# Attention with a threshold and a feed-forward block on one core: the plan's order after 47 drawn shifts of its ranks

## The chip, the core and the metric

The kernel runs on one NeuronCore of a Trainium2 chip. The metric is the time of one launch in microseconds (us) of device time. The engines are TensorE (PE in the profile; its weight loads are PEld), VectorE (DVE), ScalarE (ACT), GpSimd (POOL) and SyncE (SP, which here only issues DMAs). Each runs its own row of instructions in the order in which the program was written for it, and semaphores make one engine wait for another.

## The reference

Eight batches of eight heads, 576 positions, head width 64. An attention keeps only those scores that lie within `tau` of their row's maximum; its output, 4608 tokens of width 512, goes through two matrix products of inner width 2048 with `s * relu(h)^2 + b` between them. The inputs q, k, v and w_in are drawn eight times larger than the setup shows.

```python
scores = scale * np.matmul(q, k.transpose(0, 1, 3, 2))
thresh = np.max(scores, axis=-1, keepdims=True) - tau
scores = np.where(scores >= thresh, scores, -1000000000.0)
scores = scores - np.max(scores, axis=-1, keepdims=True)
attn = np.exp(scores)
attn = attn / (np.sum(attn, axis=-1, keepdims=True) + 1e-09)
attn_out = np.matmul(attn, v)
...
h = x @ w_in
r = np.maximum(h, 0.0)
g = s * (r * r) + b
out = g @ w_out
```

## The kernel before

**Attention, by visits and tiles.** A visit is a pair of heads with 256 query rows (half of a batch; in the second half 64 rows more, the tail). There are 64 visits. A visit has four tiles of 128 query rows of one head, with a tail five; tiles are numbered from 0 through the whole run, so tiles 0 to 3 are visit 0, and 16 to 20 visit 4. A tile goes through these steps:

- TensorE makes the scores of the two heads of a tile pair (L368; later visits use split numbers, L379 and L390). They go to one of three PSUM tiles, s0, s1 and o, in turn.
- DVE scales them in place and takes the row's extreme (L411), ACT takes the exponential into a buffer em0, em1, tr0 or tr1 (L422), DVE cuts by the threshold and sums (L425) and takes the reciprocal (L428), POOL multiplies by it (L429).
- In the first eight visits TensorE transposes the result (L439 into the score's own PSUM tile, and four times L441 into the tiles h or pv), and ACT copies it to er (L448, L450). Later DVE transposes (L462, L464), and DMAs carry the blocks to er.
- When all tiles of a visit are in er, TensorE multiplies by the values (L492, into pv), and ACT copies the result into the token block x (L502).

**Feed-forward, by blocks and steps.** Four visits fill a block of 256 tokens (18 blocks, two of them made of the tails). ACT and DVE split it into a high and a low part (L599, L601). Step f of 16 makes one slice of the inner width: twelve products (L615, into h), ReLU and square on ACT (L622, L623), a split into high and low part (ACT L625 and POOL L626, gl), and two times three products with w_out (L632, into o).

**Weights.** Each of the 16 slices of weights is loaded once by DMA as 64-bit words and turned into two 32-bit parts during the first 155 us: ACT L560, DVE L563 and L565, ACT L569, POOL L571, each once for w_in and once for w_out, and a sum on DVE (L574). So the first block's step f can't start before slice f is there.

**The order.** Nothing here is scheduled on the chip. Every operation is handed to a `Plan` (L32) with its engine, a cost, and the keys that it reads and writes. `ordered` (L121) is a list scheduler: it runs a model of the engines and takes on each the ready operation of lowest rank. `run` (L61) tries 18 settings, in eight rounds each; a round schedules forward, then backward from the end, and the backward starts are the next ranks. `worth` plays each forward order with random delays, and the order of the lowest mean wins. The operations are then written in that order, all engines in one list, and from this list the framework derives the semaphore waits. It does so by whole tiles: an operation that touches s0 waits for the last one before it in the list that touched s0, even where the plan's keys keep the two apart (the transposition L439 writes columns of s0 that the scaling L411 does not read).

Of the kernel before, what the change touches and what calls it, by code (L numbers as in the profile page):

```python
# [26 lines left out]
FIRST_WEIGHTS = 4  # L27
SECOND = 3.5
PAIR = 1170


class Plan:  # L32
# [28 lines left out]
    def run(self):  # L61
        ops = self.ops
        after = [[] for _ in ops]
        for n, o in enumerate(ops):
            for d in o[4]:
                after[d].append(n)
        before = [o[4] for o in ops]
        best = None
        for share, later, stretch in [(a, b, c) for a in self.SHARES for b in self.LATER for c in self.STRETCH]:
            rank, early = [o[5] for o in ops], set()  # L70
            for _ in range(ROUNDS):
                more = [(share if n in early else later) * self.SPARE.get(o[0], 0) +
                        (stretch - 1) * o[1] * (o[0] == "PE" and n in early) for n, o in enumerate(ops)]
                busy = [o[1] + s for o, s in zip(ops, more)]
                done = [o[2] + s for o, s in zip(ops, more)]
                order = self.ordered(before, after, rank, busy, done, False)
                worth = self.worth(order)
                if best is None or worth < best[0]:
                    best = worth, order
                early = {n for t, n in order if t < self.EARLY}  # L80
                end = {n: t + done[n] for t, n in order}
                last = max(end.values())
                order = self.ordered(after, before, [last - end[n] for n in range(len(ops))], busy, done, True)
                start = {n: -t - done[n] for t, n in order}
                rank = [start[n] for n in range(len(ops))]
        self.order = best[1]
        return [ops[n][3] for _, n in self.order]

    def worth(self, order):
        return sum(self.played(order, *slow) for slow in self.SLOW) / len(self.SLOW)  # L90
# [100 lines left out]
def tile_attention_ffn(ctx: ExitStack, tc: tile.TileContext, qT, kT, v, tau, w_in, w_out, s, b, out):  # L191
# [56 lines left out]
    def pe(cost, fn, r, w, at, tiled=False):  # L248
        plan.add("PE", (cost, cost + 170), fn, r, w, at, tiled=tiled)
# [101 lines left out]
    def scores(vs, i, t):  # L351
# [11 lines left out]
        def pairs():  # L363
            for hf in range(2):
                cs = slice(hf * HS, (hf + 1) * HS)
                for j in range(2):
                    r = slice(j * D, (j + 1) * D)
                    nc.tensor.matmul(flat[ks[j]][:, S0 + hf * HS:S0 + (hf + 1) * HS], qr[r, n, t * P:(t + 1) * P], kr[r, n, cs],  # L368
                                     start=True, stop=True)
        pe(PAIR, pairs, vs.kq + ["guard"] + (["h0"] if not i else []), ks, i - SCORES_AHEAD, True)  # L370

# [472 lines left out]
```

## Time and profile before

| | us |
|---|---|
| median of 3 runs | 1227.43 |
| lowest and highest | 1227.29, 1227.7 |
| the profiled execution | 1229.16 |
| its span, first to last instruction | 1227.2 |

| engine | busy us | share of the span |
|---|---|---|
| PE | 1198.6 | 98% |
| PEld | 987.3 | 80% |
| DVE | 798.6 | 65% |
| ACT | 765.1 | 62% |
| POOL | 718.3 | 59% |

The profiled execution took 1.96 us more than its span; that lies before the first and behind the last instruction. Share of busy time is over the whole span. A stretch of the run can be limited by another engine than the one that is busiest over the whole. A wait stands in brackets behind an instruction: how long its engine was idle just before it, and what released it.

### The profile page before, as it was taken

The numbers are of one execution on the slowest core, as the hardware profiler recorded it, in microseconds if no ns is written. First come the engines' busy times: TensorE is split into PE (matmuls) and PEld (weight loads), VectorE is DVE, ScalarE is ACT, GpSimd is POOL, SyncE is SP. The second block draws the span as 40 slices with busy tenths as digits, with TensorE's granted clock in tenths as the row PEclk, the third lists the DMA queues.
The fourth block names the chain that finished last, engine by engine and source line by source line (L and its number), as shares of the span: only waits on it lengthen the run. The fifth ranks groups of instructions, "written<-read, shape, count | busy, mean of one in ns | idle before, by whom it ended". The sixth has DMA issues, their size and how long they took to land.

```text
span 1227.2 us, 24552 instructions
## 1 busy us (share of the span) xinstructions
PE 1198.6 (98%) x7926; PEld 987.3 (80%) x7926; DVE 798.6 (65%) x2158; ACT 765.1 (62%) x1890; POOL 718.3 (59%) x822
## 2 busy tenths in 40 slices
PE   7779999999999999999999999999999999999998
PEld 5457777887887888888888888888888888878987
DVE  6897876767777766657676757666666576663021
ACT  5777755666666666656666666666656665654443
POOL 3777745767765775656665665667656676652200
PEclk7899999999999999999999999999999999999999
DMA  7851165777777776676576766566866666752000
GB/s 248 270 194 45 39 152 137 164 185 170 185 169 172 172 171 163 164 166 163 131 178 155 169 155 155 132 156 154 185 146 163 159 156 149 174 134 64 9 18 18
DMA packets 259536, 180.67 MB, mean 147 GB/s; under 512 B 83537, under 2 KB 238161, under 8 KB 259409
## 3 DMA queue, kind: packets, MB, share of 16 engines
q1 hardware_dynamic: 259120, 178.98, 60.1%
q8 instruction: 63, 1.03, 0.4%
q14 instruction: 65, 0.52, 0.1%
q10 hardware_dynamic: 288, 0.13, 0.0%
HBM read 87.03 MB, written 9.44 MB: 79 GB/s over the span
## 4 chain that ended last, share of the span: by engine, by line
PE 93%; DMA 2%; DVE 2%; ACT 1%; issue 1%; POOL 1%; SPq 0%; ACTq 0%; DVEq 0%; POOLq 0%
PE h L615 34%; PE o L632 32%; PE pv L492 13%; PE s L379 9%; PE s L368 2%; PE s L390 1%; PE pv L441 1%; DVE s L411 1%; DMA tau_t<-in_tau_dram 1%; DMA vb<-in_v_dram 1%; DMA qr<-in_q_dram 0%; DMA w<-in_moe_w_out_dram 0%; PE s L357 0%; PE s L439 0%; ACT em L422 0%
## 5 line engine op out<-in xcount | busy, mean ns | idle before, releaser
L615 PE MATMUL h<-xh,w 128*128 128x256 f32 x2304 | 467.1, 284 | 2.5 <-ACT g L622 2.5
L615 PEld LDWEIGHTS h<-xh,w 128*128 128x128 f32 x2304 | 377.5, 190 | 29.4 <-issue 11.2
L632 PE MATMUL o<-w,gh 128*128 128x512 f32 x1152 | 365.5, 399 | 0.6 <-DVE em L652 0.6
L411 DVE TENSOR_SCALAR_CACHE_REDUCE s<-s,nsc 128x576 f32<-128x576 f32 x283 | 230.7, 821 | 161.4 <-PE s L379 123.7
L429 POOL TENSOR_SCALAR em<-em,st,zero 128x576 f32<-128x576 f32 x270 | 229.5, 851 | 178.2 <-DVE st L428 123.2
L615 PE MATMUL h<-xl,w 128*128 128x256 f32 x1152 | 325.2, 282 | 0.6 <-DVE xl L601 0.6
L626 POOL TENSOR_TENSOR gl<-g,gh 128x256 fp32r<-128x256 f32 x272 | 204.0, 751 | 185.5 <-ACT gh L625 164.0
L425 DVE SCALAR_TENSOR_TENSOR em<-s,st,em 128x577 f32<-128x577 f32 x268 | 216.9, 810 | 77.1 <-ACT st L420 48.9
L422 ACT ACTIVATE em<-s,st 128x576 f32<-128x576 f32 x268 | 197.6, 738 | 70.5 <-DVE s L411 44.0
L632 PEld LDWEIGHTS o<-w,gh 128*128 128x128 f32 x1152 | 196.6, 189 | 37.3 <-issue 11.9
L632 PE MATMUL o<-w,gl 128*128 128x512 f32 x576 | 224.7, 390 | 0.6 <-POOL gl L626 0.6
L615 PEld LDWEIGHTS h<-xl,w 128*128 128x128 f32 x1152 | 219.0, 190 | 6.4 <-DVE xl L601 0.8
L622 ACT ACTIVATE g<-h 128x256 f32<-128x256 f32 x288 | 110.2, 383 | 172.4 <-PE h L615 151.5
L462 DVE STREAM_TRANSPOSE tr<-em 128x512 f32<-128x512 f32 x252 | 178.0, 706 | 53.5 <-POOL em L429 42.1
L492 PE MATMUL pv<-er,vb 128*64 128x256 f32 (+1 forms) x1280 | 174.2, 418 | 3.4 <-ACT er L450 3.4
L344 POOL TENSOR_TENSOR k<-kr,k 64x576 fp32r<-64x576 f32 x104 | 148.5, 1429 | 45.6 <-ACT k L343 31.5
L492 PEld LDWEIGHTS pv<-er,vb 128*64 128x64 f32 x1280 | 86.9, 139 | 74.0 <-issue 14.8
L625 ACT CAST gh<-g 128x256 fp32r<-128x256 f32 x288 | 116.3, 404 | 43.3 <-PE o L632 40.2
L379 PE MATMUL s<-k 128*128 128x288 f32 x832 | 142.8, 296 | 0.2
L379 PEld LDWEIGHTS s<-k 128*128 128x128 f32 x832 | 126.9, 188 | 15.2 <-issue 2.1
L632 PEld LDWEIGHTS o<-w,gl 128*128 128x128 f32 x576 | 108.2, 188 | 25.8 <-POOL gl L626 1.3
L623 ACT ACTIVATE g<-g 128x256 f32<-128x256 f32 x288 | 120.0, 417 | 4.3
(104 smaller groups left out, 945.5 us busy)
## 6 DMA issues: line engine op xcount, KB each, us to landing
er<-tr SPq DMA_DIRECT2D x448, 160.0 KB, 3.4
kr<-in_k_dram SPq DMA_DIRECT2D x116, 288.0 KB, 4.2
vb<-in_v_dram SPq DMA_DIRECT2D x128, 128.0 KB, 3.0
qr<-in_q_dram SPq DMA_DIRECT2D x56, 160.0 KB, 4.4
er<-tr SPq DMA_DIRECT2D x112, 80.0 KB, 2.3
w<-in_moe_w_in_dram SPq DMA_DIRECT2D x16, 512.0 KB, 6.0
w<-in_moe_w_out_dram SPq DMA_DIRECT2D x16, 512.0 KB, 6.1
out_dram<-oo SPq DMA_DIRECT2D x30, 256.0 KB, 2.6
```

Of the source, the lines that this page charges most:

```text
L344: pool((1500, 1500), lambda: nc.gpsimd.tensor_tensor(out=z()[D:P], in0=kr[D:P, j], in1=z()[D:P].bitcast(F32), op=ALU.subtract), rk + [("z" ...
L379: nc.tensor.matmul(flat[sk][:, S0 + hf * HS:S0 + (hf + 1) * HS], lazy["q"][:, x, j, qc], lazy["k"][:, j, cs], start=(x == 0), stop=(x == 1))
L411: dve((740, 875), lambda: nc.vector.tensor_scalar(out=ps[:, S0:S0 + S], in0=ps[:, S0:S0 + S], scalar1=nsc, scalar2=None, op0=ALU.mult, op1 ...
L422: act((632, 740), lambda: nc.scalar.activation(out=ev, in_=ps[:, S0:S0 + S], func=AF.Exp, bias=st8[:, 0:1], scale=-1.0), [sk, (ks_, 0)], [ ...
L425: dve((742, 830), lambda: nc.vector.scalar_tensor_tensor(out=eb, in0=ps[:, S0:S0 + S + 1], scalar=st8[:, 1:2], in1=eb, op0=ALU.is_le, op1= ...
L429: pool((795, 825), lambda: nc.gpsimd.tensor_scalar(out=ev, in0=ev, scalar1=st8[:, 4:5], scalar2=zero, op0=ALU.mult, op1=ALU.add), [em_k, ( ...
L462: nc.vector.transpose(out=to[:, :, 0:NQ].rearrange("p m c q -> p m (c q)"), in_=ev[:, 0:M].rearrange("p (m r) -> p m r", m=4))
L492: nc.tensor.matmul(ps[j * D:(j + 1) * D, 0:32 * nb], vb[r, n, j, c], er[r, n, j, 0:nb, 32 * c:32 * c + 32], start=(c == 0), stop=(c == 4))
L615: nc.tensor.matmul(ps, w[:, c, :], x[:, c, :], start=(c == 0 and i == 0), stop=(c == NC - 1 and i == 2))
L623: act((322, 417), lambda: nc.scalar.activation(out=g, in_=g, func=AF.Square), [f"g{k}"], [f"g{k}"], at)
L626: do((712, 740), lambda: eng.tensor_tensor(out=lo, in0=g, in1=hi.bitcast(F32), op=ALU.subtract), [f"g{k}", f"gh{n}"], [f"gl{n}"], at)
L632: nc.tensor.matmul(bank["o"][:, t, :], a[:, ts_], w, start=(f == 0 and i == 0), stop=(f == NF - 1 and i == 2))
```

## The change

The order that won is taken up once more with the ranks that made it. For each of 47 numbers, `shifted` seeds a random generator, draws a width and a start of a stretch of the model's time, some kinds of operations (a kind is an engine, a cost and a place in the code), and a shift; the ranks of the operations of those kinds in that stretch are shifted by it, all alike or each by its own draw. `ordered` makes a new order, and the next number shifts that one. The last order is used without a comparison. Costs, keys, tiles and the operations themselves are the same. A line of the kernel before stands 21 lines further on behind the new function (L411 is L432, L571 is L592).

```diff
+SHIFTS = (0, 20, 48, 103, 150, 205, 238, 276, 352, 398, 411, 419, 421, 471, 481, 540, 551, 662, 694, 892, 1084, 1250,
...
-                    best = worth, order
+                    best = worth, order, rank, busy, done
...
-        self.order = best[1]
+        worth, order, rank, busy, done = best
+        for n in SHIFTS:
+            rank = self.shifted(n, order, rank)
+            order = self.ordered(before, after, rank, busy, done, False)
+        self.order = order
         return [ops[n][3] for _, n in self.order]
+
+    def shifted(self, n, order, rank):
+        draw, end = random.Random(n), order[-1][0]
+        kind = [(o[0], o[1], o[3].__code__.co_firstlineno) for o in self.ops]
+        kinds = sorted(set(kind))
+        width = draw.choice((2e3, 5e3, 15e3, 50e3, 200e3))
+        first = draw.uniform(0, 150e3) if draw.random() < 0.4 else draw.uniform(0, end)
+        some = set(draw.sample(kinds, draw.choice((1, 1, 1, 2, 4)))) if draw.random() < 0.75 else set(kinds)
+        shift, alike = draw.gauss(0, 1) * draw.choice((500, 2000, 6000)), draw.random() < 0.6
+        new = list(rank)
+        for t, m in order:
+            if first <= t < first + width and kind[m] in some:
+                new[m] += shift if alike else draw.gauss(0, 1) * shift
+        return new
```

Each engine still runs the same instructions: 7071 matrix products on PE, of which 1701 stand at another place of its row than before; the first 58 and the last 541 places are unchanged. On DVE 686 of 1584 places differ, on POOL 236 of 827. Three places follow.

DVE in the second visit (tiles 6 to 9 pass through; L563 and L565 convert weights), before:

```order
L425 SCALAR_TENSOR_TENSOR tr0_79,st0_71<-s0_98,st0_71,tr0_79 128x577
L425 SCALAR_TENSOR_TENSOR tr1_80,st1_72<-s1_99,st1_72,tr1_80 128x577
L563 TENSOR_SCALAR xl_172<-xl_172 128x512
L565 SCALAR_TENSOR_TENSOR k_87<-w2_153,k_87 128x512
L565 SCALAR_TENSOR_TENSOR xl_172<-w1_138,xl_172 128x512
L563 TENSOR_SCALAR k_87<-k_87 128x512 x2
L565 SCALAR_TENSOR_TENSOR k_87<-w2_153,k_87 128x512
L411 TENSOR_SCALAR o_100,st2_73<-o_100,nsc_68 128x576
L411 TENSOR_SCALAR s0_98,st3_74<-s0_98,nsc_68 128x576
L416 TENSOR_SCALAR st2_73<-st2_73,tau8_67 128x1
L428 RECIPROCAL st0_71<-st0_71 128x1
L428 RECIPROCAL st1_72<-st1_72 128x1
```

and now:

```order
L446 SCALAR_TENSOR_TENSOR tr0_79,st0_71<-s0_98,st0_71,tr0_79 128x577
L586 SCALAR_TENSOR_TENSOR xl_172<-w1_138,xl_172 128x512
L446 SCALAR_TENSOR_TENSOR tr1_80,st1_72<-s1_99,st1_72,tr1_80 128x577
L449 RECIPROCAL st0_71<-st0_71 128x1
L449 RECIPROCAL st1_72<-st1_72 128x1
L584 TENSOR_SCALAR k_87<-k_87 128x512
L432 TENSOR_SCALAR o_100,st2_73<-o_100,nsc_68 128x576
L586 SCALAR_TENSOR_TENSOR xl_172<-w1_138,xl_172 128x512
L437 TENSOR_SCALAR st2_73<-st2_73,tau8_67 128x1
L432 TENSOR_SCALAR s0_98,st3_74<-s0_98,nsc_68 128x576
```

The block of six conversions that stood between the second visit's cuts and the next scalings is spread out, and the reciprocals of tiles 6 and 7 follow their cuts at once.

PE at the same place (the scores of tiles 8 and 9, the values of visit 0, the transpositions of tiles 5, em1, and 6, tr0), before:

```order
L439 MATMUL s1_99<-k_87,em0_77 64x128
L441 MATMUL h_102<-k_87,em0_77 128x128 x4
L492 MATMUL pv_101<-er_84,vb_83 64x256 x10
L368 MATMUL o_100<-kr_81,qr_82 128x288
L368 MATMUL s0_98<-kr_81,qr_82 128x288
L368 MATMUL o_100<-kr_81,qr_82 128x288
L368 MATMUL s0_98<-kr_81,qr_82 128x288
L439 MATMUL o_100<-k_87,em1_78 64x128
L441 MATMUL pv_101<-k_87,em1_78 128x128 x4
L439 MATMUL s0_98<-k_87,tr0_79 64x128
L441 MATMUL h_102<-k_87,tr0_79 128x128 x4
```

and now:

```order
L460 MATMUL s1_99<-k_87,em0_77 64x128
L462 MATMUL h_102<-k_87,em0_77 128x128 x4
L389 MATMUL o_100<-kr_81,qr_82 128x288
L389 MATMUL s0_98<-kr_81,qr_82 128x288
L389 MATMUL o_100<-kr_81,qr_82 128x288
L389 MATMUL s0_98<-kr_81,qr_82 128x288
L513 MATMUL pv_101<-er_84,vb_83 64x256 x10
L460 MATMUL s0_98<-k_87,tr0_79 64x128
L462 MATMUL h_102<-k_87,tr0_79 128x128 x4
L460 MATMUL o_100<-k_87,em1_78 64x128
L462 MATMUL pv_101<-k_87,em1_78 128x128 x4
```

The scores stand ahead of the values now, and tile 6 is transposed ahead of tile 5.

POOL at the first steps of the first feed-forward block (tiles 18, tr0, 19, tr1, and 20, em0; gl0 and gl1 of steps 0 and 1), before:

```order
L571 TENSOR_TENSOR w7_657<-k_87,w7_657 128x512 x2
L429 TENSOR_SCALAR tr1_80<-tr1_80,st1_72,zero_69 128x576
L429 TENSOR_SCALAR em0_77<-em0_77,st2_73,zero_69 128x576
L626 TENSOR_TENSOR gl0_95<-g0_90,gh0_92 128x256
L626 TENSOR_TENSOR gl1_96<-g1_91,gh1_93 128x256
L571 TENSOR_TENSOR w8_736<-k_87,w8_736 128x512 x2
```

and now:

```order
L592 TENSOR_TENSOR w7_649<-k_87,w7_649 128x512
L647 TENSOR_TENSOR gl0_95<-g0_90,gh0_92 128x256
L647 TENSOR_TENSOR gl1_96<-g1_91,gh1_93 128x256
L450 TENSOR_SCALAR tr1_80<-tr1_80,st1_72,zero_69 128x576
L450 TENSOR_SCALAR em0_77<-em0_77,st2_73,zero_69 128x576
L647 TENSOR_TENSOR gl2_97<-g0_90,gh2_94 128x256
```

The low parts of the first two steps stand ahead of the multiplications of tiles 19 and 20.

## Rows read from the trace of the kernel before

**Rows 1.** The page: PE's total, and its granted clock in 40 equal slices
```profile
PE 1198.6 (98%) x7926; PEld 987.3 (80%) x7926; DVE 798.6 (65%) x2158; ACT 765.1 (62%) x1890; POOL 718.3 (59%) x822
...
PEclk7899999999999999999999999999999999999999
```

**Rows 2.** Windows: stretch, length, busy us and count by engine, PE clock, DMA
```profile
0.00:90.00 90.00, 68.06 (x367) 44.02 (x369) 73.41 (x199) 59.85 (x127) 53.87 (x59) 0.83 0.74 242
90.00:1227.00 1137.00, 1130.52 (x7563) 943.29 (x7557) 725.14 (x1960) 705.26 (x1764) 664.39 (x764) 1.00 0.60 140
50.00:60.00 10.00, 8.98 (x45) 4.58 (x43) 9.05 (x24) 6.95 (x17) 6.52 (x6) 0.68 0.85 276
```

**Rows 3.** Timeline of PE, 24 to 72 us: start, length, instruction, idle before
```profile
26.56 2.53 PE L492 MATMUL pv<-er,vb 128*64 128x256 f32 x20 [0.30 <-ACT er L450]
...
35.24 0.30 PE L439 MATMUL s<-k,tr 128*64 128x128 f32 x1 [4.32 <-POOL tr L429]
...
43.38 1.24 PE L368 MATMUL s<-kr,qr 64*128 64x288 f32 x8
...
50.97 4.73 PE L492 MATMUL pv<-er,vb 128*64 128x256 f32 x20 [0.21 <-ACT er L450]
...
63.46 4.06 PE L492 MATMUL pv<-er,vb 128*64 128x256 f32 x20 [1.94 <-ACT er L450]
...
71.19 0.36 PE L615 MATMUL h<-xh,w 128*128 128x256 f32 x1
```

**Rows 4.** Timeline of DVE, 24 to 71 us
```profile
24.85 0.82 DVE L411 TENSOR_SCALAR_CACHE_REDUCE s<-s,nsc 128x576 f32<-128x576 f32 x1 [0.96 <-PE s L439]
...
38.59 0.83 DVE L411 TENSOR_SCALAR_CACHE_REDUCE s<-s,nsc 128x576 f32<-128x576 f32 x1 [1.50 <-PE s L439]
...
51.78 0.42 DVE L563 TENSOR_SCALAR k<-k 128x512 int32<-128x512 int32 x1
...
52.98 1.43 DVE L563 TENSOR_SCALAR k<-k 128x512 int32<-128x512 int32 x1
...
57.01 0.82 DVE L425 SCALAR_TENSOR_TENSOR tr<-s,st,tr 128x577 f32<-128x577 f32 x1 [0.92 <-ACT er L448]
...
61.12 0.82 DVE L411 TENSOR_SCALAR_CACHE_REDUCE s<-s,nsc 128x576 f32<-128x576 f32 x1 [1.09 <-PE s L439]
...
68.95 0.83 DVE L411 TENSOR_SCALAR_CACHE_REDUCE s<-s,nsc 128x576 f32<-128x576 f32 x1 [1.79 <-PE s L439]
...
70.74 1.95 DVE L601 TENSOR_TENSOR xl<-x,xh 128x512 fp32r<-128x512 f32 x2
```

**Rows 5.** Timeline of POOL, 31 to 56 us
```profile
31.11 1.61 POOL L571 TENSOR_TENSOR w<-xl,w 128x512 fp32r<-128x512 f32 x1 [3.22 <-ACT w L569]
...
52.87 2.67 POOL L571 TENSOR_TENSOR w<-k,w 128x512 fp32r<-128x512 f32 x2
```

**Rows 6.** Timeline of ACT, the copy of visit 2's output
```profile
55.75 0.37 ACT L502 COPY x<-pv 128x256 f32<-128x256 f32 x1 [2.75 <-PE pv L492]
```

**Rows 7.** Timeline of PE, the first feed-forward steps
```profile
82.20 0.30 PE L439 MATMUL s<-k,tr 128*64 128x128 f32 x1 [0.83 <-POOL tr L429]
...
83.97 0.50 PE L632 MATMUL o<-w,gl 128*128 128x512 f32 x1 [0.56 <-POOL gl L626]
```

**Rows 8.** Timelines of POOL and of PE, the last slice of weights and its step
```profile
150.12 2.50 POOL L571 TENSOR_TENSOR w<-k,w 128x512 fp32r<-128x512 f32 x2
...
153.49 0.28 PE L615 MATMUL h<-xh,w 128*128 128x256 f32 x1
```

**Rows 9.** Timeline of PE near 300 us: scores, values, scores, products, without a wait
```profile
300.69 0.70 PE L379 MATMUL s<-k 128*128 128x288 f32 x4
301.32 2.38 PE L492 MATMUL pv<-er,vb 128*64 128x256 f32 x20
...
305.16 0.70 PE L379 MATMUL s<-k 128*128 128x288 f32 x4
305.70 0.63 PE L632 MATMUL o<-w,gh 128*128 128x512 f32 x2
```

More of the change, by code (lines that the diff above doesn't have):

```diff
@@ L29 @@
 PAIR = 1170
+SHIFTS = (0, 20, 48, 103, 150, 205, 238, 276, 352, 398, 411, 419, 421, 471, 481, 540, 551, 662, 694, 892, 1084, 1250,
+          1275, 1299, 1778, 1780, 1798, 1801, 1870, 1872, 1930, 2001, 2079, 2081, 2158, 2254, 2325, 2554,
+          2669, 3110, 3156, 3307, 3437, 3536, 3712, 3722, 3857)
 class Plan:
```

## The prediction, as recorded before the run

> **What bounds the kernel now.** I read the page first: TensorE is busy for 98% of the span [rows 1]. The windows then split the run in two [rows 2]. From 90 us on PE is busy for 1130.5 of 1137.0 us at a granted clock of 1.00; there it is the bound, and since every product stays, another order can win nothing but switches between shapes. In the first 90 us it is busy for 68.1 us at 0.83, and much of that busy time is stretched by the lower of the clock's two levels: the values of a visit took 2.53 us at 26.56, but 4.73 us at 50.97 and 4.06 us at 63.46 [rows 3]. So the question is how soon PE gets dense work, that is, when the first product of the feed-forward starts: 71.19 us [rows 3]. What comes after is a dense row of PE work, nearly the same in both kernels, and ends as much earlier as it starts earlier.
>
> What sets 71.19? VectorE is busy for 73.4 of the 90 us [rows 2]. I counted its row in both programs ahead of the first L601, which makes the low part that the first step waits for: 20 scalings, 18 cuts, 18 reciprocals, 15 L565 and 6 sums in both; the new row has 16 L563 for 15 and two of the small L416 fewer. DVE's work ahead of the feed-forward is thus the same, and its start can move only by DVE's waits and by how far its instructions are stretched. From 24 us on the waits that matter are five: 0.96, 1.50, 0.92, 1.09 and 1.79 us, together 6.26 us [rows 4]. Up to 22 us the rows of DVE, PE, ACT and POOL are the same.
>
> **Part A, waits ahead of the feed-forward.** In three of the five a scaling L411 waits for a transposition L439, of which it needs nothing: it touches the same PSUM tile, and the list has it first. In the new program the scalings of tiles 6, 8, 9, 10, 12, 16 and 17 name their scores alone; the transposition now comes behind them, waits for them, and the exponential of the same tile waits for it. I walked the new rows by hand from 24 us, with the duration of each instruction from the trace where nothing stretched it.
>
> - Tile 6 (0.96 us of wait before) starts when its scores end, 0.35 us after DVE is free. The transposition of tile 3 comes behind it, that of tile 4 later still, and the scaling of tile 7 waits 1.3 us for that.
> - POOL before stood for 3.22 us behind a conversion, then made two weight products ahead of tile 6 [rows 5], and PE stood 4.32 us for that multiplication [rows 3]. In the new row tiles 6 and 7 come ahead of both. That wait of PE goes; the 1.50 us at 38.59, which hung on it, go with it. In their place the cut of tile 9 waits 1.7 us for its exponential, since ACT has a copy in front that waits for the scores of tile 11, and tile 11 waits 0.45 us for a copy.
> - The 0.92 us at 57.01 came from ACT, which kept the exponential of tile 15 behind the copy of visit 2's values, 2.75 us of waiting [rows 6]. The new row has that exponential in front: gone. The 1.09 us at 61.12 go too, since tile 16 no longer waits for the transposition of tile 15, which hung on POOL.
> - The 1.79 us at 68.95 stay, at 1.75 us: the scaling of tile 18 waits for scores that stand behind the last values of the block.
>
> The waits add to 0.35 + 1.3 + 1.7 + 0.45 + 1.75 = 5.55 us instead of 6.26: 0.7 us won. The walk itself puts the first L601 at 68.05 us instead of 70.74, 2.7 us earlier; the other 2.0 us are stretched instructions of the old run, which the walk lacks. The clearest is an L563 that took 1.43 us at 52.98 beside a weight product of POOL that began at 52.87; the one at 51.78 took 0.42 us [rows 4, 5]. Whether the new order meets POOL less often, the trace of before can't show. So A lies between -0.7 us (stretched as before) and -2.7 us (not at all); about the middle, **-1.8 us**, since the row of POOL is as full as before and its pieces are only moved.
>
> The Trainium skill ("SBUF — State Buffer", "SBUF: two separate sides") says that a VectorE instruction with two SBUF inputs, or in a two-port mode, and a GpSimd one lock a shared port pair for a whole instruction, and the loser waits. The 1.43 us agree. By that rule spreading six conversions among POOL's multiplications makes as many meetings as before, and A would be -0.7 us.
>
> **Part B, the first steps of the feed-forward.** Between 71 and 90 us PE waits twice for POOL: 0.83 us for tile 19 and 0.56 us for gl0 [rows 7]. In the new row gl0 and gl1 stand ahead of tiles 19 and 20, and PE has step 3 in front of tile 19's transposition. Both waits can go (-1.4 us) or be followed by others (0, since DVE releases tile 19 in any case and PE gets there sooner). I take **-1.0 us**.
>
> **Part C, switches.** PE changes between products on the whole array and on parts of it 182 times before and 180 times after. From the scores at 300.69 to the values behind them 0.63 us pass, from those at 305.16 to a whole product 0.54 us [rows 9]: 0.09 us for a change in, and I take the same for one out. Two fewer: **-0.2 us**.
>
> **What is moved and costs nothing.** After 90 us some 1600 products of PE change places by a few us of its work. DVE, ACT and POOL have a third of their time free there [rows 1], which hides it. The one cover that is thin is the weights: the last slice of w_in is ready when POOL ends at 152.62, and its step starts at 153.49, 0.87 us later [rows 8]. In the new PE row that step stands 2.0 us of PE work further to the front, and with A and B it would start 4.8 us earlier. POOL's product for it stands about 1.7 us of POOL's work earlier, DVE's conversion about 2.6 us of DVE's. If these engines gain A as well, the slice comes 3.5 to 4.4 us earlier, and PE waits 0 to 0.4 us; if they gain nothing through A, about 2 us. I take 0 and keep +2 for the range. DMA issues move only among themselves; no wait on the way to 71 us named above was for a load.
>
> **The sum** against the profiled execution's own 1229.16 us: -1.8 - 1.0 - 0.2 = -3.0, 1226.2 us. The runs' median, 1227.43 us, lies 1.7 us below that execution; the difference goes onto it: **1224.4 us**.
>
> **Rivals.**
>
> 1. *The gain is eaten.* DVE meets POOL as often as before (A -0.7), the waits of B move on (0), and the step of the last slice waits up to 2 us. For it: POOL's fill and the thin cover of 0.87 us. Against it: PE's 4.32 us have a cause that is plainly gone. -0.7 - 0.2, plus 0 to 2: 1226.5 to 1228.5 us, no change.
> 2. *TensorE's low clock, slower.* Scores, scaling, transposition, exponential and cut of one PSUM tile now form one chain through PE, where DVE before ran ahead of two of these links or had them behind it. My walk has PE at the full level. The scores of a tile pair took 1.24 us at 43.38 [rows 3]; in the ratio of the values, 4.73 to 2.53, the low level makes that 2.3 us, and the transpositions behind them some 0.5 us longer, 1.6 us in all on the chain (an estimate from these rows). The last values would take 4.06 instead of 2.53 us, 1.5 us more. The stretch from 50 to 60 us was at 0.68 [rows 2]. If all of visits 1 to 3 run low, A is -1.8 + 3 x 1.6 + 1.5 = +4.5, and the whole, with C alone, +4.3: 1231.7 us. It decides the sign once more than about two of the three visits run low. The Trainium skill ("TensorE: Matmul & The Clock Gate", Part 1) says that the low level is the default and that activity ends it; the rows agree in that PE has 1.00 once it is dense, and by that rule PE's new pieces of waiting (0.9 us behind tile 6, 1 us around tile 9) speak for this rival and the lost 4.32 us against it.
> 3. *More than forecast.* All five old waits go without new ones, nothing is stretched, and both waits of B go: A down to -4, B -1.4, C -0.2: 1221.8 us. Against it are the new waits that the walk finds.
>
> **How the numbers follow.** The measurement can tell 0.2% from no change, 2.45 us: below 1224.98 is faster, above 1229.88 slower. The forecast lies only just on the faster side. Forecast (1223 to 1225) 0.42; more than forecast 0.14; rival 1, and a forecast that falls short by a us, 0.31; rival 2 0.13. So faster 0.56, same 0.31, slower 0.13. The range takes in rival 3's 1221.8 with a margin for its low end and rival 1's 1228.5: 1221.0 to 1229.0; outside it lie most of rival 2 and a little below, less than 0.2.
>
> **What would show it.** In the profile of the changed kernel: the first L615 at about 69.4 us (A); no wait of PE of over 2 us between 25 and 50 us; no wait of DVE at the cut of tile 15; the scalings of tiles 6, 10 and 16 without a transposition as releaser, but a wait at the cut of tile 9; gl0's product without a wait (B); no new wait of PE at L615 around 140 to 155 us; and from 90 us on PE as dense as now. The forecast is wrong if L601 starts at 70 us or later, if the clock from 30 to 60 us is lower than before, or if PE shows waits for weights.

## The result

The changed kernel is **slower**: 1237.96 us (1237.79 to 1239.06, five runs) against 1227.70 us (1227.29 to 1231.55, five runs) for the kernel before on the same chip. The ratio is 1.0076, 95% interval 1.0064 to 1.0089: 9.3 us more (by 1227.4) where 3.0 us less was forecast, and over the top of the range, 1229.0. The ratios here and in the next section leave out two executions in which the chip was disturbed (1901 us of rest_only and 3039 us of the kernel before), while the medians are over all.

The page of the changed kernel, against [rows 1]: the totals and PE's clock in 40 slices.

```profile
span 1236.1 us, 24530 instructions
...
PE 1204.9 (97%) x7926; PEld 990.9 (80%) x7926; DVE 801.1 (65%) x2158; ACT 764.7 (62%) x1890; POOL 716.0 (58%) x822
...
PEclk7789999999999999999999999999999999999999
```

The same number of instructions on each engine, and PE busy 6.3 us longer; the low clock lasts one slice longer. The timeline of PE (start, length, instruction, idle before), against [rows 3], puts most of it ahead of the feed-forward:

```profile
57.14 4.43 PE L513 MATMUL pv<-er,vb 128*64 128x256 f32 x20
...
69.42 4.73 PE L513 MATMUL pv<-er,vb 128*64 128x256 f32 x20 [3.47 <-ACT er L471]
74.08 2.29 PE L389 MATMUL s<-kr,qr 64*128 64x288 f32 x8
...
78.66 0.36 PE L636 MATMUL h<-xh,w 128*128 128x256 f32 x1
```

PE's last products, before (the first line) and now:

```profile
1222.50 0.40 PE L632 MATMUL o<-w,gl 128*128 128x512 f32 x1
...
1230.24 0.40 PE L653 MATMUL o<-w,gl 128*128 128x512 f32 x1
```

The first product of the feed-forward starts at 78.66 us, not 71.19: 7.47 us of the span's 8.9. From there to the end of PE's last product 1152.0 us pass, before 1151.7. The last 1.2 us lie behind PE's last product, where the results are stored (5.4 us to the end of the span, before 4.3). So where the start goes the end goes, as the prediction had it; the start went the other way. DVE's waits of over a microsecond from 24 us to that point, against [rows 4]:

```profile
26.71 0.83 DVE L432 TENSOR_SCALAR_CACHE_REDUCE s<-s,nsc 128x576 f32<-128x576 f32 x1 [1.63 <-PE s L460]
...
38.22 0.82 DVE L446 SCALAR_TENSOR_TENSOR em<-s,st,em 128x577 f32<-128x577 f32 x1 [3.32 <-ACT em L443]
...
49.01 0.83 DVE L432 TENSOR_SCALAR_CACHE_REDUCE s<-s,nsc 128x576 f32<-128x576 f32 x1 [1.52 <-PE s L460]
...
63.90 0.83 DVE L432 TENSOR_SCALAR_CACHE_REDUCE s<-s,nsc 128x576 f32<-128x576 f32 x1 [1.64 <-PE s L389]
...
68.29 0.82 DVE L446 SCALAR_TENSOR_TENSOR em<-s,st,em 128x577 f32<-128x577 f32 x1 [1.69 <-ACT er L469]
...
77.05 0.83 DVE L432 TENSOR_SCALAR_CACHE_REDUCE s<-s,nsc 128x576 f32<-128x576 f32 x1 [4.12 <-ACT er L469]
```

They add to 13.92 us; the five of [rows 4] add to 6.26. The difference, 7.66 us, is the delay of the start but for 0.2 us. DVE's work ahead of the feed-forward is nearly unchanged (from 24 us to L622 it took 40.6 us without its waits, from 24 us to L601 before 40.2), so its waits account for the delay of the start, and the question is what makes them.

**Where the waits come from.** A tile of the scores is used by four engines: PE writes the scores and later the 64x128 transposition (L439, now L460) into it, DVE scales in place and cuts, ACT reads it for the exponential and copies the transposition out (L448, now L469). Any two of these that follow each other in the list on one tile are ordered by a semaphore, whichever columns they touch. (The Trainium skill, "PSUM — Partial Sum Buffer", "PSUM bank collisions raise a hardware error", says that such accesses of two engines to one 2 KiB bank have to be kept apart by bank, in the simple version of its rule, and not by address. The program keeps them apart by tile; no run here lets them meet.) The list decides who waits. Read out of both programs:

| on one tile | before | now |
|---|---|---|
| scaling of 6 (9, 10, 16), transposition of 3 (6, 7, 15) | of 6, 10 and 16 the scaling waits for the transposition | in all four the transposition waits for the scaling, and the exponential or the cut of that tile for the transposition |
| copy L448/L469 of tile 13, scores of 17 | the scores wait for the copy | the copy waits for the scores |

The second line is seen in ACT's timeline, and it sets the end of the stretch:

```profile
61.62 0.37 ACT L523 COPY x<-pv 128x256 f32<-128x256 f32 x1 [2.82 <-PE pv L513]
63.94 0.26 ACT L469 COPY er<-s 64x128 f32<-64x128 f32 x1 [1.95 <-PE s L389]
...
68.78 0.58 ACT L471 COPY er<-pv 128x512 f32<-128x512 f32 x1
```

The copy of tile 13 stands until the scores of tiles 16 and 17 are made, and these stand on PE behind the values of visit 2 (57.14, 4.43 us at the low clock). Behind that copy ACT has the other copies of visit 3; the last starts at 68.78. The values of visit 3 wait 3.47 us for it, take 4.73 us, and behind them come the scores of tiles 18 and 19 in 2.29 us, a transposition, its copy on ACT (76.76), the scaling of tile 18 that waited 4.12 us for that copy, and then L622, for which the feed-forward waits. Two of these links, the copy of tile 13 behind the scores and the scaling of tile 18 behind a copy, exist only because different pieces share a PSUM tile.

### The profile page after: what moved, and what is told of

The parts are those of the page before. It is cut to its first block, busy times and chain, and to the rows that moved or that the text cites. A ratio compares the mean times of both kernels' runs of the same rounds, so it can differ in the third digit from the quotient of the medians.

```text
span 1236.1 us, 24530 instructions
## 1 busy us (share of the span) xinstructions
PE 1204.9 (97%) x7926; PEld 990.9 (80%) x7926; DVE 801.1 (65%) x2158; ACT 764.7 (62%) x1890; POOL 716.0 (58%) x822
## 4 chain that ended last, share of the span: by engine, by line
PE 95%; DVE 2%; issue 1%; ACT 1%; DMA 1%; POOL 0%; ACTq 0%; DVEq 0%
PE h L636 34%; PE o L653 33%; PE pv L513 14%; PE s L400 9%; PE s L389 2%; PE s L411 1%; PE pv L462 1%; DVE s L432 1%; DMA tau_t<-in_tau_dram 1%; DVE em L446 0%; PE s L460 0%; PE o L389 0%; PE s L378 0%; DVE o L432 0%; DVE tr L446 0%
## 5 line engine op out<-in xcount | busy, mean ns | idle before, releaser
L636 PE MATMUL h<-xh,w 128*128 128x256 f32 x2304 | 467.2, 284 | 1.0 <-ACT g L643 1.0
L636 PEld LDWEIGHTS h<-xh,w 128*128 128x128 f32 x2304 | 377.7, 190 | 28.1 <-issue 9.4
L432 DVE TENSOR_SCALAR_CACHE_REDUCE s<-s,nsc 128x576 f32<-128x576 f32 x283 | 230.2, 820 | 160.7 <-PE s L400 122.4
L636 PE MATMUL h<-xl,w 128*128 128x256 f32 x1152 | 325.4, 282 | 0.3 <-DVE xl L622 0.3
L450 POOL TENSOR_SCALAR em<-em,st,zero 128x576 f32<-128x576 f32 x270 | 226.2, 838 | 151.8 <-DVE st L449 114.2
L636 PEld LDWEIGHTS h<-xl,w 128*128 128x128 f32 x1152 | 219.1, 190 | 7.2 <-DVE xl L622 0.5
L513 PE MATMUL pv<-er,vb 128*64 128x256 f32 (+1 forms) x1280 | 177.3, 424 | 3.5 <-ACT er L471 3.5
L646 ACT CAST gh<-g 128x256 fp32r<-128x256 f32 x288 | 116.1, 404 | 43.7 <-PE o L653 40.6
```

Of the source, the lines that this page charges most:

```text
L432: dve((740, 875), lambda: nc.vector.tensor_scalar(out=ps[:, S0:S0 + S], in0=ps[:, S0:S0 + S], scalar1=nsc, scalar2=None, op0=ALU.mult, op1 ...
L450: pool((795, 825), lambda: nc.gpsimd.tensor_scalar(out=ev, in0=ev, scalar1=st8[:, 4:5], scalar2=zero, op0=ALU.mult, op1=ALU.add), [em_k, ( ...
L513: nc.tensor.matmul(ps[j * D:(j + 1) * D, 0:32 * nb], vb[r, n, j, c], er[r, n, j, 0:nb, 32 * c:32 * c + 32], start=(c == 0), stop=(c == 4))
L636: nc.tensor.matmul(ps, w[:, c, :], x[:, c, :], start=(c == 0 and i == 0), stop=(c == NC - 1 and i == 2))
```

## The experiments

Each kernel's ratio is to the kernel before, run beside it on the same chip. 0.1% is 1.2 us. After the new function and the edits, line numbers shift again; names don't.

| kernel | us | before, us | ratio, 95% interval | first step, us |
|---|---|---|---|---|
| changed kernel | 1237.96 | 1227.70 | 1.0076 (1.0064 to 1.0089) | 78.66 |
| start_only | 1236.65 | 1228.31 | 1.0064 (1.0047 to 1.0080) | 75.45 |
| rest_only | 1230.80 | 1228.31 | 1.0017 (1.0005 to 1.0028) | 74.49 |
| before_free | 1224.29 | 1228.31 | 0.9962 (0.9947 to 0.9977) | 66.87 |
| after_free | 1223.58 | 1228.31 | 0.9957 (0.9942 to 0.9972) | 67.03 |
| upto_892 | 1229.36 | 1228.30 | 1.0000 (0.9988 to 1.0011) | 73.80 |
| upto_1798 | 1234.09 | 1228.30 | 1.0038 (1.0025 to 1.0051) | 75.87 |
| after_flip | 1235.06 | 1228.30 | 1.0047 (1.0034 to 1.0061) | 73.83 |
| aware_shifts | 1226.60 | 1228.30 | 0.9983 (0.9972 to 0.9993) | 70.30 |
| after_warm | 1238.18 | 1229.48 | 1.0074 (1.0052 to 1.0095) | 78.27 |
| before_warm | 1229.35 | 1229.48 | 1.0000 (0.9990 to 1.0011) | 71.28 |
| aware_warm | 1228.30 | 1229.48 | 0.9992 (0.9979 to 1.0004) | 66.66 |
| aware_early | 1224.13 | 1229.48 | 0.9955 (0.9938 to 0.9971) | 66.51 |
| after_warm2 | 1236.11 | 1229.24 | 1.0052 (1.0038 to 1.0065) | 73.92 |
| rest_late | 1233.99 | 1229.24 | 1.0036 (1.0022 to 1.0051) | 73.30 |
| start_late | 1236.36 | 1229.24 | 1.0056 (1.0044 to 1.0069) | 79.05 |

The first step is of one profiled execution and is a rough guide only: start_only, start_late and the changed kernel have the same rows up to there, and so have rest_only, rest_late and the kernel before, yet they differ by up to 3.6 and by up to 3.3 us. The ratios decide.

**1. Which half of the order?** The lists of before and after are cut at 80 us of the plan's time and spliced.

```diff
-        self.order = order
+        first = [(t, n) for t, n in order if t < 80e3]
+        there = {n for _, n in first}
+        self.order = first + [(t, n) for t, n in plain if n not in there]
```

> The new order up to 80 us of the plan's own time (all that stands ahead of the feed-forward and its first steps), then the old order for the rest of the program. Theory A (the loss is made ahead of the feed-forward): the first L636 starts at about 78.5 us as in the changed kernel, and the time is some 7.5 us over the kernel before, 1235. Theory C (the loss is made in the dense part, by later weights and new waits): 1228 to 1229 us.

> The other half: the old order up to 80 us of the plan's time, then the new one. Theory A: the first product of the feed-forward starts at 71.2 us as before, and only the 1.5 us remain that the two traces differ by behind it: about 1229 us, at most 1230. Theory C: 1235 us or more.

The start alone costs 7.9 us, the rest alone 2.1, together 10.0 against 9.3 for the whole. Theory A holds for some four fifths of the loss. rest_only's 1230.80 us lie over theory A's 1230 and far under theory C's 1235.

Where its 2.1 us lie is not shown. Up to the first step its rows are those of the kernel before, yet in its profiled execution that step comes 3.3 us later, and from there to PE's last product 1151.4 us pass, not more than the 1151.7 before. start_only has both a later first step (4.3 us) and a longer stretch behind it (1154.5 us), though its order there is the old one; the splice may have made that. In the changed kernel itself this stretch grew by 0.3 us.

```profile
74.49 0.56 PE L639 MATMUL h<-xh,w 128*128 128x256 f32 x1
...
1225.54 0.40 PE L656 MATMUL o<-w,gl 128*128 128x512 f32 x1
```

**2. The shared tile taken away.**

```diff
-                nc.tensor.transpose(out=tt, in_=ev[:, M:S], identity=ident)
+                nc.tensor.transpose(out=tp[0:T, 0], in_=ev[:, M:S], identity=ident)
...
-                    out=e[0:T, NQ], in_=tt[:, c0:c1].rearrange(...)), [kt], ke, i + 0.5)
+                    out=e[0:T, NQ], in_=ident[0:T, c0:c1].rearrange(...)), [kt], ke, i + 0.5)
```

> The kernel before, with the 64x128 transposition L439 written into the bank of the other four (its copy L448 then reads the identity instead, so the values of the last 64 keys are left out): nothing but scores lies in the banks of the scores, and no scaling waits for a transposition, nor an exponential, with the engines' rows unchanged. Theory A: the waits of 0.96 and 1.09 us at L411 go, and the first L615 starts 1 to 3 us earlier: 1224.5 to 1226.5 us. If the shared banks are of no account: 1227.4.

> The same in the changed kernel, whose rows stay as they are. Theory A1 (the chain of scaling, transposition, exponential and cut through one PSUM tile makes the loss): the waits of 3.32 us at the cut of tile 9 and of 4.12 us at the scaling of tile 18 go or fall below 2 us, the clock from 30 to 80 us rises, the first L636 starts at 69 to 71.5 us, and the time is 1227 to 1229.5. Theory A2 (the new row of PE itself, with its pieces of waiting, keeps the clock low, whatever the banks): the values at 45, 57 and 69 us still take over 3.7 us, the first L636 starts at 76 us or later, and the time stays above 1234.

The engines run the same rows, and the loss is gone: without the shared tile the changed kernel falls by 14.6 us of the 1227.4 (1.0076 to 0.9957), the kernel before by 4.7, a little more than was expected. Theory A1 holds, and by more than it said (1223.58 us, where it had 1227 at the least). DVE's waits in after_free, all of over half a microsecond from 24 us to the first step:

```profile
55.35 0.82 DVE L432 TENSOR_SCALAR_CACHE_REDUCE s<-s,nsc 128x576 f32<-128x576 f32 x1 [0.75 <-PE s L389]
...
64.97 0.83 DVE L432 TENSOR_SCALAR_CACHE_REDUCE s<-s,nsc 128x576 f32<-128x576 f32 x1 [1.49 <-PE s L389]
```

The 3.32 and the 4.12 us are gone. PE's granted clock (the third number from the right) from 30 to 60 us is 1.00, 0.96 and 0.84, where the changed kernel has 0.81, 0.66 and 0.71 (its windows stand under 5):

```profile
30.00:40.00 10.00, 7.64 (x53) 4.61 (x54) 9.80 (x27) 7.04 (x16) 9.11 (x7) 1.00 0.85 276
40.00:50.00 10.00, 5.92 (x38) 3.58 (x39) 10.00 (x25) 8.54 (x20) 5.41 (x5) 0.96 0.93 305
50.00:60.00 10.00, 6.53 (x39) 3.45 (x37) 9.25 (x23) 7.51 (x17) 8.53 (x6) 0.84 0.66 218
```

PE's values of visits 2 and 3 are still slow there, the last one 4.14 us after a wait of 2.89, and yet the first step comes at 67.03:

```profile
59.63 4.14 PE L513 MATMUL pv<-er,vb 128*64 128x256 f32 x20 [2.89 <-ACT er L471]
...
67.03 0.36 PE L636 MATMUL h<-xh,w 128*128 128x256 f32 x1
```

Freed of the shared tile, the two orders end within 0.6 us of each other, less than their intervals. The 3 us that the new order was forecast to win can't be seen even there. (The copy that reads the identity no longer waits for the transposition at all, so part of the gain of both is that; how much was not measured.)

**3. Which shifts, and which way round?** The list of 47 is cut short, or five pairs of the list are turned round with every engine's row kept.

```diff
-SHIFTS = (0, 20, 48, ..., 892, 1084, 1250, 1275, 1299, 1778, 1780, 1798, 1801, ..., 3857)
+SHIFTS = (0, 20, 48, ..., 892)                                              # upto_892
+SHIFTS = (0, 20, 48, ..., 892, 1084, 1250, 1275, 1299, 1778, 1780, 1798)    # upto_1798
...
-        self.order = order
+        self.order = self.flipped(order)     # transpositions of 3, 6, 7, 12, 15 ahead of scalings of 6, 9, 10, 15, 16
```

> The first 20 of the 47 shifts, up to the one named 892. Of the scalings of tiles 6 to 18 only those of tiles 9, 13 and 15 stand in the list ahead of the transposition they share a bank with (9 and 15 before, seven in the changed kernel). If the loss comes with those meetings: the first L636 starts at 70 to 73 us, and the time is 1226 to 1229 us. If it comes with any reordering of the dense part: over 1230.

> The first 27 shifts, up to 1798: now with 1250 and 1778, which put the scalings of tiles 6 and 8 ahead of the transpositions of tiles 3 and 5 as well (six such pairs). If the loss comes with the meetings in the shared banks, this stands between: the first L636 at 73 to 76 us, 1230 to 1234 us. If one later shift (1801, 2554 or 3110) makes it all: 1227 to 1229.

> The changed kernel with the same row on every engine; in the list alone, five transpositions (of tiles 3, 6, 7, 12 and 15) now come ahead of the scalings (of tiles 6, 9, 10, 15 and 16) that they share a bank with, so that the scaling waits for the transposition, as in the kernel before, and not the other way round. If the direction of the wait makes the loss (the chain through PE): first L636 at 71 to 74 us, 1228 to 1232 us. If the rows themselves make it, in which these pieces meet in one bank whichever waits: 1235 us or more.

With one way of waiting, the loss grows with the number of scalings of tiles 6 to 18 that the list has ahead of the transposition on their tile: two in the kernel before, three in upto_892 (1.0000), five in upto_1798 (1.0038; the six of the expectation count tile 19 too), seven in the changed kernel (1.0076). (The times of upto_892 and upto_1798 lie 0.4 and 0.1 us over their first ranges.) The last 20 shifts also move other things, so this is a dose that fits, not a proof for each pair. Turning the five pairs round gives back 3.6 us of the 9.3 and leaves 5.8: the time, 1235.06 us, is at the lower edge of the second expectation, the first step at 73.83 us within the first. So the direction of the wait matters. How much of the 5.8 us the pieces cost by meeting on one tile whichever of them waits, this run can't tell, for it leaves other meetings as they were: the scalings of tiles 8 and 12 still stand ahead of a transposition, and the scaling of tile 18 still waits for a copy:

```profile
72.22 0.83 DVE L474 TENSOR_SCALAR_CACHE_REDUCE s<-s,nsc 128x576 f32<-128x576 f32 x1 [3.78 <-ACT er L511]
```

**4. A plan that knows of the tiles.** In `ordered` and in `played`, an operation on s0, s1 or o starts no sooner than those ahead of it in the list on that tile have ended (on other engines, reads against reads left free). Then shifts are drawn anew and kept if the sum of the plays falls.

```diff
+    def held(self, n, t, held):
+        to = self.ops[n][0]
+        for k, m in self.banks[n]:
+            wrote, read = held.get(k, (None, ()))
+            for e, end in ([wrote] if wrote else []) + (list(read) if m else []):
+                if e != to:
+                    t = max(t, end + (150 if to == "PE" else 50))
+        return t
...
+            if not back:
+                t = self.held(n, t, held)
+                self.hold(n, t + done[n], held)
             order.append((t, n))
```

> A planner that knows of the shared banks: each piece that writes or reads a bank of the scores is placed and weighed behind those that stand ahead of it in the list, and 47 shifts are drawn anew and kept by that sum (with PE's pieces ahead of 75 us 1.0 to 1.5 times as long). Its own sum, counted with the banks, gives a first product of the feed-forward 1.5 us sooner than that of the kernel before at the full clock and 5 us sooner with pieces 1.5 times as long. If the waits for the banks are what the plan lacked: it beats the kernel before, 1221 to 1226 us. If the sum misses more than the banks: 1227 us or more.

> The plan that knows of the shared banks with 31 more shifts, drawn over the first 85 us of the plan's time alone and kept by the same sum (twelve plays at PE pieces 1.0 to 1.7 times as long). Counted with the banks, the first product of the feed-forward comes 2.2 us sooner than with the 47 at every clock, and the end 1.7 us. If that sum is now complete enough to go by: 1223.5 to 1226 us. If it misses as much as it finds: 1226 to 1229 us.

Both beat the kernel before: by 2.1 us, and with the 31 further shifts by 5.5 us, the first 0.6 us over its range (1226.6 us, between its two theories), the second inside it. aware_early leaves no work out and is the fastest kernel here that doesn't. From 24 us to its first step DVE has one wait of over 0.6 us:

```profile
31.15 0.83 DVE L457 TENSOR_SCALAR_CACHE_REDUCE o<-o,nsc 128x576 f32<-128x576 f32 x1 [1.31 <-ACT er L494]
...
54.60 0.82 DVE L471 SCALAR_TENSOR_TENSOR tr<-s,st,tr 128x577 f32<-128x577 f32 x1 [0.57 <-ACT er L494]
```

The plan's own sum shows why the 47 shifts looked good. This is a sum of the program's own costs, not a time on the chip. Without the tiles it puts the changed order 6.8 us ahead (1232.4 against 1239.2); with them, at the full clock, 0.9 us ahead, and the first step some 2 us behind. So even with the tiles it doesn't show the 9.3 us: it ranks aware_shifts and aware_early rightly, and the changed order still wrongly.

**5. The clock.** Products of zeros are added where PE waits.

```diff
+                for _ in range(6 if 3 <= i < 18 else 0):
+                    nc.tensor.matmul(bank[kp[0].strip("01")][:, 0:NB], ones, gh[0], start=True, stop=True)
                 nc.tensor.transpose(out=tt, in_=ev[:, M:S], identity=ident)
```

> The changed kernel with products of zeros added that nothing reads (128x256 into a bank that the next real product overwrites), in the first four visits: ten ahead of the values of each, three ahead of each transposition of tiles 4 to 17, so that PE works where it waited. Clock theory (the low clock is what makes the bank waits long): the granted clock from 30 to 75 us rises over 0.9, the values at about 45, 57 and 69 us take 2.5 us instead of 3.7 to 4.7, and the time falls to 1229 to 1233 us. Bank theory (the waits come from the row and the shared banks, the clock only follows them): the clock rises, and the time stays within 3 us of the changed kernel, 1235 to 1240 us.

> The same products of zeros in the kernel before. Clock theory: the values at 51 and 63.5 us fall from 4.73 and 4.06 to 2.53 us, 1224 to 1226 us. Bank theory: 1227 to 1230 us, the added products cost as much as the clock gives.

> The plan that knows of the shared banks, with ten products of zeros ahead of the values of each of the first four visits alone. Its last wait of weight is 4.23 us at the scaling of tile 18, behind the last values at the low clock. Clock theory: these values fall to 2.53 us, that wait by 1.5 to 2 us, and the time to 1224 to 1225.5 us. Bank theory: 1226 to 1228 us.

> The changed kernel with six products of zeros (128x256) ahead of each transposition of tiles 3 to 17, into the bank that this transposition then overwrites as a whole; here no copy waits for them and the values stay complete. Clock theory: the granted clock from 30 to 75 us rises, the values fall towards 2.5 us, and the time to 1229 to 1233 us. Bank theory: the clock rises, and the time stays at 1235 to 1241 us.

In the first three the expectation was wrong in one point: the ten products ahead of the values overwrote transposed blocks of the next visit whose copy stood later in the list, and that copy waited for them. Their times (1.0074, 1.0000, and 0.9992 where the same plan without added products has 0.9983) thus hold that cost too, which the traces show small (one wait of 0.47 us for such products in before_warm, at 27.61 us), and that of the products (1.45 us for ten at 30.55 us in after_warm). after_warm2 has only those that the next transposition overwrites as a whole. Its windows from 20 to 60 us (stretch, length, busy by PE, PEld, DVE, ACT, POOL, PE's clock, DMA), and the same of the changed kernel:

```profile
20.00:30.00 10.00, 7.53 (x45) 4.89 (x45) 8.24 (x28) 7.56 (x16) 4.94 (x6) 0.98 0.79 252
30.00:40.00 10.00, 9.74 (x74) 7.00 (x69) 7.65 (x21) 6.31 (x15) 8.34 (x7) 1.00 0.53 153
40.00:50.00 10.00, 8.00 (x56) 5.29 (x56) 9.94 (x24) 6.48 (x14) 6.69 (x6) 1.00 0.72 239
50.00:60.00 10.00, 8.78 (x66) 6.13 (x64) 9.96 (x27) 5.69 (x13) 6.44 (x6) 1.00 0.85 280
```

```profile
20.00:30.00 10.00, 7.23 (x29) 4.73 (x28) 8.34 (x26) 7.81 (x17) 4.89 (x5) 0.67 0.81 242
30.00:40.00 10.00, 8.02 (x46) 4.35 (x46) 6.61 (x20) 5.47 (x13) 7.12 (x6) 0.81 0.46 149
40.00:50.00 10.00, 9.03 (x44) 4.99 (x44) 8.48 (x23) 5.04 (x10) 5.63 (x5) 0.66 0.56 182
50.00:60.00 10.00, 6.57 (x32) 3.94 (x34) 10.00 (x27) 7.74 (x17) 6.33 (x6) 0.71 0.91 303
```

The clock is at its upper level, the first three values take 2.53 us each, and 2.9 us of the 9.3 are won; 6.4 stay (the time, 1236.11 us, is in the range of the bank theory), with the largest waits at the same places:

```profile
37.00 0.82 DVE L446 SCALAR_TENSOR_TENSOR em<-s,st,em 128x577 f32<-128x577 f32 x1 [2.30 <-ACT em L443]
...
71.86 0.83 DVE L432 TENSOR_SCALAR_CACHE_REDUCE s<-s,nsc 128x576 f32<-128x576 f32 x1 [2.90 <-ACT er L471]
```

The last values ran slowly in this kernel too (65.44 us, 3.91 us), so a little more might be had there. In the kernel before the same device brings the clock to 1.00 from 30 us on and all four values to 2.53 us, and the time stays (1.0000), with the cost of the added products in it. So the low clock makes the waits longer and is not what makes them. 2.9 us is what the clock gave back net of what the added products cost; that cost was not measured by itself.

**6. The rest of the order.** The cut is moved to 110 us.

> The old order up to 110 us of the plan's own time, the new one behind that. If the reordering of the dense part costs something by itself (the 2 us that the cut at 80 us showed): 1229 to 1231 us. If those 2 us belong to the stretch from 80 to 110 us, where POOL's waits are: 1227.5 to 1229 us, no difference from the kernel before.

> The new order up to 110 us, then the old one. With the loss wholly ahead of that point: the time of the changed kernel, 1236.5 to 1239 us. If the dense part carries 2 us: 1235 to 1236.5 us.

Neither half gives back what the other loses, and the kernel with the new order behind 110 us is 4.4 us slower (1233.99 us, outside both expectations). That the 2 us belong to the stretch from 80 to 110 us falls. In PE's timeline rest_only and the changed kernel have a wait in common that the kernel before lacks (its longest behind 85 us is 0.58); the changed kernel's:

```profile
135.59 0.27 PE L460 MATMUL s<-k,tr 128*64 128x128 f32 x1 [1.21 <-POOL gl L647]
...
304.29 0.74 PE L653 MATMUL o<-w,gh 128*128 128x512 f32 x2 [0.84 <-DVE oo L673]
```

and rest_only's of the same transposition:

```profile
131.10 0.27 PE L463 MATMUL s<-k,tr 128*64 128x128 f32 x1 [1.23 <-POOL gl L650]
```

POOL's timeline has that low part gl end at 135.56, just ahead of the transposition; why the new order makes PE wait for it there I have not followed further. With one of 0.85 like the second of the changed kernel and a third of 0.32 us, rest_only has 2.4 us of such waits. They are not shown to be its loss: others are gone in their place, and all of PE's idle time behind the first step is 5.7 us in rest_only and 5.8 in the kernel before. rest_late has these waits and one of 1.49 us at 121 us, which the splice itself may have made, and 8.2 us of idle time in all; of its 4.4 us I can't separate the order from the splice, nor from the later first step on the old rows.

## Why the prediction was wrong

- **What bounds the kernel** was right: the stretch from the first product of the feed-forward to PE's last moved by 0.3 us, and the end followed the first product, but for 1.2 us behind PE's last. That DVE's waits set that product was right as well: +7.66 us of waits, +7.47 us of start.
- **Part A failed**, by its hand walk. The wait of PE for POOL, 4.32 us, did go (the longest from 25 to 50 us is 1.71), and so did that at the cut of tile 15, as forecast. The new ones were found in kind and missed in size: tile 7 1.63 us (1.3 in the walk), the cut of tile 9 3.32 (1.7), tile 18 4.12 (1.75). Three were not in the walk: tile 13 1.52, tile 16 1.64, the cut of tile 16 1.69. 13.92 us in place of 5.55. The other half of A, fewer stretched instructions, gave nothing: without its waits DVE took 40.6 us from 24 us on, before 40.2.
- **The step behind that** was that "in the new program the scalings [of seven tiles] name their scores alone", taken as a gain in three of five waits. A wait that leaves one side of a shared tile goes to the other. I followed it to the exponential of the same tile, and to ACT's copies at one place (tile 11, with the right mechanism); the copy of tile 13, which now waits for the scores of tile 17 with all of visit 3's copies behind it, I missed. That chain sets 69.42 and by that 78.66.
- **Durations at the full clock** were the second error of the walk: the values 4.43 and 4.73 us, the scores 2.29 us where it had 2.53 and 1.24. after_warm2 got 2.9 us of it back.
- **Rival 2** named the chain (scores, scaling, transposition, exponential, cut through one tile) and the side. Its price, +4.5 us for A, was too small, since it let the clock carry the cost: it would have been none at the full clock, where after_warm2, at that clock from 20 to 60 us, still loses 6.4. (By its own terms the sign turns sooner than it says: -3.0 + 1.6 + 1.5 is over 0 with one visit at the low clock, if that is the last.) With a chance of 0.13 it was held too low: the turned waits had been read from the new program at seven tiles, and only the clock was asked about.
- **Part B**: the two waits of [rows 7] went, as did one of 1.12 us at 78.47, and 0.48, 0.52 and 1.09 us came between 80 and 88 us. Since the stretch from the first product to the last is 0.3 us longer, nothing is left of a gain there; its other end, 0, was right. **Part C** can't be told from the rest.
- **"What is moved and costs nothing"**: the weights' cover held, as forecast: PE shows no wait at L636 from 140 to 170 us. That the moved pieces cost nothing is not borne out: rest_only's ratio says 2.1 us (0.6 to 3.4), though no trace shows where.
- Of the three wrong signs that the prediction listed two came true: L601 (now L622) at 78.57 us, over 70; and the clock from 30 to 50 us, 0.81 and 0.66 where it was 0.83 and 0.98. The third, waits for weights, did not.

## What to carry to other kernels

Where a plan's keys know less than the rules by which waits are derived, every gain of its own sum is suspect: count the tiles that two engines use for different things, and let the plan hold an operation until the one ahead of it in the list on that tile has ended. When an instruction no longer waits in a new program, look for the one that now waits for it, and walk on from there through every engine's queue, the small copies too. Take the waits away before the clock: here the granted clock rose by itself when the shared tile went (0.66 to 0.96 from 40 to 50 us), and added products that raised it gave back 2.9 of 9.3 us.

## What I had not expected

In before_warm the granted clock is 1.00 from 30 to 80 us and the values of all four visits take 2.53 us where they took up to 4.73, and the time is the same to 0.1%. That could mean that PE's speed is hidden behind waits, or that the added products cost what the clock gives; this run can't tell. Executions with the same rows speak against the first: they reach the first step up to 3.3 and 3.6 us apart, and the later the lower their clock from 20 to 70 us. On the old rows it is 71.19 us at 0.81, 73.30 at 0.77 (rest_late) and 74.49 at 0.74 (rest_only), on the new ones 75.45 at 0.77 (start_only), 78.66 and 79.05 at 0.74 (the changed kernel and start_late). These are six single executions, and such a match shows no cause. The kernel before and rest_only:

```profile
20.00:70.00 50.00, 38.01 (x210) 21.98 (x208) 43.38 (x117) 35.36 (x75) 34.18 (x28) 0.81 0.71 229
...
20.00:70.00 50.00, 38.39 (x199) 22.07 (x199) 43.20 (x114) 33.40 (x71) 32.71 (x27) 0.74 0.67 218
```

What stays open: how much the clock takes at its last slow place, where the 2.1 us of rest_only lie, and what of rest_late's 4.4 us is the splice's. A PSUM tile of its own for the transposition, with all the work left in, wasn't tried.
